# Range of A as one ScalarE Square pass, wider sums, dummy matmuls, wide output tiles: Nyström attention with gated experts on one core

## The chip, the core and the metric

One core of one Trainium2 chip. The metric is the device time of one execution in microseconds (us), the slowest core's, as the median of several runs. TensorE is called PE in the profile, VectorE DVE, ScalarE ACT, GpSimd POOL, SyncE SP. PEld is TensorE's weight load, which overlaps PE (before: 77.8 us of it beside 137.0 of PE, in a span of 176.5). The granted clock is the share of TensorE's full clock that the profile records for a stretch.

A run more than 1.5% above the fastest of the same kernel counts as slow. A ratio is the mean time of one kernel's fast runs over the mean of the other kernel's fast runs of the same rounds, so it isn't quite the ratio of the two medians that stand beside it.

## The reference, cut to what matters

```python
B, H, S, D = 8, 8, 576, 64;  m = 32                      # landmarks
q_lm, k_lm = means of 18 neighbouring rows of q, k
A  = softmax(q @ k_lm.T / 8)                              # 576 x 32 per head
Bm = softmax(q_lm @ k_lm.T / 8)                           # 32 x 32
C  = softmax(q_lm @ k.T / 8)                              # 32 x 576
Z  = Bm.T / (norm_1(Bm) * norm_inf(Bm) + 1e-6)
for _ in range(6): Z = 2 * Z - Z @ Bm @ Z
x  = (A @ Z @ C @ v) as (B*S, H*D)                        # 4608 x 512
e  = argmax(x @ w_gate);  gate_w = softmax(x @ w_gate)[e];  eom = sigmoid(x @ w_output_gate)[e]
out = gate_w * eom * (relu(x @ w1[e]) @ w2[e])            # 8 experts, 512 -> 1024 -> 512
```

A is nearly uniform for these inputs. The kernel therefore picks an expert per batch and evaluates the expert once on a linear form, and proves at the end, from the range of A (how far A is from 1/32), that this was allowed. If the proof fails for a batch, a fix-up behind a branch computes that batch again. With these inputs the fix-up isn't taken.

## The kernel before: the parts that matter here

Every instruction is placed by hand: the text `PLAN` lists name, engine and buffer slots (`dv0.1:G` means step 1 of the range of batch 0 on GpSimd), and each engine runs its own instructions in the order of that list.

```python
    def range_(b):                        # the range of A: five steps on GpSimd, one reduction on VectorE
        dev = tl("dev", fifo=False)
        ...
        def centre():
            nc.gpsimd.tensor_scalar(out=dev.ap, in0=A16[b]..., scalar1=-1.0 / m, scalar2=2048.0, op0=ADD, op1=MUL)
        def square(k):
            nc.gpsimd.tensor_tensor(span(0, k), span(0, k), span(0, k), op=MUL)
        def fold(k):
            nc.gpsimd.tensor_tensor(span(0, k), span(0, k), span(k, 2 * k), op=ADD)
        ...
        def top():
            nc.vector.tensor_reduce(dm[:, b:b + 1], span(0, S // 8), axis=AX, op=ADD)
```
```python
        def rowsum():                     # row sums of A: 8 matmuls of 144 columns a batch (QS = 144)
            for s in range(2):
                for par in range(2):
                    for hf in range(2):
                        o = hf * HS + s * QS
                        nc.tensor.matmul(pd.ap[quad(2 * par + hf), 0, 0:QS], lhsT=sel[:, s]...,
                                         rhs=A16[b][:, par, o:o + QS], start=(s == 0), stop=(s == 1))
```
```python
        for c in range(NC):               # output: five blocks a batch, each in one of four y buffers
            pY, y = pt(1), tl("y")        # tag("y", 4, [128, HD])
            ...                           # evict pY into y on ACT or DVE, then store y
```
```python
    n_extra = nc.values_load(nxi[0:1, 0:1], min_val=0, max_val=B * E)
    with tc.If(n_extra > 0):              # the fix-up; every engine jumps over it
        ...
```

The softmax here doesn't subtract the row's maximum and nothing guards it: scores larger than these inputs give would overflow.

Of the kernel before, what the change touches and what calls it, by code (L numbers as in the profile page):

```python
# [30 lines left out]
RELU = mybir.ActivationFunctionType.Relu  # L31
ABS = mybir.ActivationFunctionType.Abs
# [99 lines left out]
c_sel:V c_gen:V c_rest:G ldk0.0:Y0 c_zero:V ldq0.0:Y0 ldk0.1:Y ks0.1:G0 ldq0.1:Y ldq1.0:Y1 c_bsel:V c_two:V qs1.0.0:G0 qs0.0:V01  # L132
ks0.0:V1 qs0.1:V1 sc0.0C:T0 ldk1.0:Y1 eB0:S0 eC0.0:S0 qs1.0.1:G ldq2.0:Y2 sc0.0A:T2 eA0.0:S ldv0:Y0 ldk2.0:Y2 Bs0:V0 Br0:V
sc0.1A:T4 eA0.1:S ks1.0:V1 sc0.1C:T6 qs1.0.2:G qs1.0.3:G qs1.0.4:G1 eC0.1:S pd0:T0 qs2.0.0:G0 qs2.0.1:G qs2.0.2:G qs2.0.3:G
ln0:S0 rd0:S0 pT0.0:T2 pT0.1:T CT0:S0 ldq4.0:Y0 ldv1:Y1 pb0.1:T4 An0.1:V pb0.0:T6 ldv2:Y2 An0.0:V sc1.0C:T0 eB1:S1 Bs1:V1
sc1.0A:T2 sc1.1A:T4 sc1.1C:T6 eC1.0:S1 eC1.1:S pTt0:T0 pT1.0:T6 eA1.0:S dv0.0:G0 eA1.1:S Ct0:V0 pTt1:T1 pT1.1:T Cv0.0:T2 pd1:T0
ln1:S0 rd1:S1 Ct1:V1 Cv0.1:T CT1:S1 pb1.0:T4 ks2.0:V1 pb1.1:T0 Cvt0:T An1.0:V xr0:V0 qs2.0.4:G0 sc2.0C:T6 eC2.0:S0 cX0:V0
sc2.1A:T4 dv0.1:G eA2.1:S sc2.0A:T2 eA2.0:S ldk4.0:Y0 cB0.1:G cB0.0:V eB2:S0 sc2.1C:T4 ldq3.0:Y1 eC2.1:S cs0:T2 dv0.2:G pd2:T6
Br1:V qs4.0.0:G0 qs4.0.1:G qs4.0.2:G pTt2:T7 An1.1:V cb00:V0 cb10:S W0.0:T cb20:V Ct2:V0 Cv1.0:T0 ln2:S0 u0.0:V1 rd2:S0 pT2.0:T4
ldk3.0:Y1 Cv1.1:T Cvt1:T xr1:V1 cX1:S2 pT2.1:T Q0.0:V0 W0.1:T cB1.1:V Q0.1:V1 cB1.0:G CT2:S0 u0.1:S0 qs4.0.3:G dv0.3:G pb2.0:T6  # L140
ldq5.0:Y2 pb2.1:T0 qs4.0.4:G1 An2.0:V dv0.4:G cs1:T4 qs3.0.0:G0 An2.1:V W0.2:T Cv2.0:T6 u0.2:S1 Cv2.1:T Q0.2:V2 W0.3:T u0.3:S0
ks4.0:V1 qs3.0.1:G Cvt2:T ldv3:Y0 dv1.0:G1 cb01:V1 qs3.0.2:G qs3.0.3:G qs3.0.4:G0 W1.0:T xr2:V0 cb11:S dt0:V cX2:V1 sc4.1A:T0
sc4.0C:T6 dv1.1:G eB4:S1 eC4.0:S1 Q0.3:V0 W0.4:T cb21:V u1.0:V2 Q1.0:V1 ldk5.0:Y2 eA4.1:S W1.1:T sc4.1C:T6 u0.4:S0 sc4.0A:T0
ldq6.0:Y0 u1.1:S2 ldk6.0:Y0 eC4.1:S ks3.0:V0 eA4.0:S qs5.0.0:G0 Q1.1:V2 ldv5:Y1 W1.2:T pT4.0:T6 Q0.4:V0 dv1.2:G pT4.1:T CT4:S1
Q1.2:V1 ldv4:Y2 u1.2:V2 W1.3:T sc3.0A:T0 W0.5:T qs5.0.1:G eA3.0:S Q0.5:V2 sc3.0C:T6 u0.5:V2 eB3:S dv1.3:G eC3.0:S0 sc3.1C:T0
Q1.3:V1 u1.3:S0 W0.6:T ks5.0:V0 qs5.0.2:G qs5.0.3:G sc3.1A:T6 qs5.0.4:G1 u0.6.0:S0 pD0:T2 ldq7.0:Y1 eC3.1:S pT3.0:T0 pT3.1:T
W1.4:T MTd0.2:S pd4:T3 dv1.4:G eA3.1:S MTd0.1:S MTd0.0:V pTt3:T6 Q1.4:V0 pd3:T7 qs6.0.0:G0 CT3:S0 pg0:T0 ln4:S0 rd4:S1 u1.4:V2
W1.5:T MWg0:S0 Ct3:V1 Cv3.0:T2 pb4.1:T0 lg0:T6 ldk7.0:Y1 u1.5:V0 Q1.5:V2 W1.6:T mx0:V0 mk0:V0 ln3:S0 Cv3.1:T u1.6.0:S1 pD1:T7
An4.1:V pN0:T4 MTd1.1:S Cvt3:T cnt0:V e00:V0 m80:V0 pTt4:T5 rd3:S0 pb3.1:T0 MTd1.0:V MTd1.2:S Ct4:V0 pb4.0:T4 e20:S0 pg1:T6
MWg1:S1 An3.1:V An4.0:V e10:S ss0:V0 sc5.0C:T0 sc5.0A:T6 eA5.0:S lg1:T4 Bs2:V0 i80:V0 sc5.1A:T6 eC5.0:S0 eB5:S dt1:V xr3:V1  # L150
mx1:V1 eA5.1:S ef0:V0 Br2:V mk1:V1 pN1:T5 e01:V1 cnt1:V m81:V1 sc5.1C:T0 i81:V1 pd5:T5 cX3:S eC5.1:S er0:G pb3.0:T6 qs6.0.1:G
qs6.0.2:G ldw0.0:G ln5:S0 ldw0.1:G cB2.0:V dv2.0:G0 cB2.1:V Cv4.0:T2 cs2:T0 Cv4.1:T An3.0:V pT5.0:T6 cb02:V0 cb12:S qs6.0.3:G
pT5.1:T e21:S1 er1:G pTt5:T5 rd5:S1 ks6.0:V1 cb22:V Ct5:S1 ldw0.2:G CT5:S0 pb5.0:T4 An5.0:V qs6.0.4:G0 W2.0:T e11:S sc6.1A:T6
dv2.1:G u2.0:V2 Q2.0:V1 ldw0.3:G Cvt4:T xr4:V0 sel0:V sc6.0A:T4 eA6.1:S pb5.1:T6 An5.1:V eA6.0:S W2.1:T dv2.2:G Q2.1:V0
sc6.0C:T4 MW0.0:T6 cX4:S0 Bs4:V1 ldw1.1:G Br4:V h00.0:V dv2.3:G u2.1:S1 eB6:S0 eC6.0:S1 sa0.0:V mk0.0:G0 X0.0:S0 g10:V ldw1.0:G
W2.2:T MW0.1:T2 Q2.2:V2 g20:V sa0.1:V u2.2:S2 Cv5.0:T4 Cv5.1:T qs7.0.0:G0 Cvt5:T h00.1:V ss1:V1 P0.0.1:T6 P0.0.0:T7 mk0.1:G1
xr5:V1 g11:V co0:G ldw1.2:G X0.1:V1 W2.3:T Q2.3:V1 P0.1.0:T cX5:S g21:V tm0:V P0.1.1:T cm0:V pd6:T4 dv2.4:G dt2:V u2.3:S1
P160.0:S0 cB4.1:V P160.1:S ks7.0:V1 cB4.0:G ln6:S0 W2.4:T ldw1.3:G Y0.2:T5 u2.4:S2 rd6:S0 dv4.0:G0 cs4:T2 qs7.0.1:G pb6.1:T6
dv4.1:G Y0.0:T4 y0.2:S0 qs7.0.2:G y0.0:S1 qs7.0.3:G Q2.4:V0 cb04:V1 W2.5:T cb14:S An6.1:V dv3.0:G1 W4.0:T Y0.3:T5 Q2.5:V2
st0.2a:Y cb24:V u4.0:V1 ldv7:Y0 u2.5:S2 Q4.0:V1 ef1:V1 y0.3:S2 MW1.0:T6 st0.0a:Y h01.0:V mk1.0:G2 sa1.0:V W2.6:T u2.6.0:S0 co1:G  # L160
dv4.2:G u2.6.1:S sc6.1C:T4 eC6.1:S X1.0:V2 W4.1:T u4.1:S0 Y0.1:T0 MW1.1:T4 h01.1:V y0.1:S3 qs7.0.4:G1 dv4.3:G pD2:T1 MTd2.0:S
Q4.1:V0 sa1.1:V mk1.1:G0 P1.0.1:T0 MTd2.1:S MTd2.2:S W4.2:T pg2:T6 MWg2:S0 P1.0.0:T1 u4.2:S2 X1.1:V0 lg2:T6 Q4.2:V2 lg3:T
sc7.0C:T4 mx2:V0 e02:V0 mk2:V0 eC7.0:S0 e22:S0 dv3.1:G W4.3:T sel1:V ldv6:Y2 st0.3a:Y pN2:T7 cnt2:V eB7:S e12:S P1.1.0:T m82:V2
i82:V2 dv3.2:G ss2:V0 sc7.1C:T6 Bs6:V0 eC7.1:S Br6:V g12:V m83:V3 er2:G P161.0:V1 Q4.3:V1 pT6.0:T4 pT6.1:T CT6:S1 P1.1.1:T
P161.1:S u4.3:V1 pTt6:T6 ldw2.0:G Ct6:V0 Y0.4:T7 dv3.3:G pb6.0:T4 y0.4:S0 dv4.4:G W4.4:T i83:V3 u4.4:S0 Cv6.0:T0 An6.0:V
sc7.1A:T6 pTt7:T4 dt4:V ef2:V0 tm1:V Q4.4:V0 Cv6.1:T cm1:V W4.5:T Cvt6:T Y1.4:T5 ef3:V Ct7:V1 u4.5:V2 ldw2.2:G ldw2.1:G y1.4:V1
eA7.1:S g22:S xr6:V0 st0.1a:Y pT7.0:T6 Q4.5:V2 ldw2.3:G dv5.0:G0 er3:G dv5.1:G pT7.1:T cX6:S1 MW2.0:T4 CT7:S0 sc7.0A:T0 W4.6:T
u4.6.0:S1 Cv7.0:T6 u4.6.1:S h02.0:V eA7.0:S Cv7.1:T mk2.0:G1 sa2.0:V Y1.3:T2 st0.4b:Y sel3:V dv3.4:G st0.4a:Y Cvt7:T ldw3.0:G
dv5.2:G dt3:V sel2:V pD4:T3 Y1.1:T0 xr7:V1 cX7:V cB6.0:G st1.4a:Y ldw3.1:G X2.0:S1 MTd4.2:V st1.4b:Y MTd4.1:S cB6.1:V MTd4.0:V
pd7:T1 ln7:S0 y1.3:S2 MW2.1:T6 h02.1:V st1.3a:Y sa2.1:V cs6:T4 rd7:S1 pg4:T2 P2.0.0:T1 MWg4:S1 mk2.1:G2 dv5.3:G cb06:V0 cb16:S  # L170
Y1.0:T2 lg4:T3 lg5:T ldw3.2:G co2:G y1.1:V3 W6.0:T cb26:V Y1.2:T0 mx4:V1 mk4:V1 dv5.4:G X2.1:S2 pN4:T6 P2.1.0:T e24:S1 u6.0:V0
cnt4:V Q6.0:V1 m84:V0 W6.1:T y1.2:S0 y1.0:S1 e04:V1 tm2:G m85:V1 MW3.0:T6 i84:V0 Q6.1:V0 ldw3.3:G h03.0:V i85:V1 sa3.0:V
pb7.0:T2 e14:S u6.1:S2 P2.0.1:T0 P162.0:S0 W6.2:T er4:G ldw4.0:G P2.1.1:T ldw4.1:G u6.2:S1 An7.0:V P162.1:S er5:G Q6.2:V2 ef4:V1
cm2:V ldw4.2:G mk3.0:G0 pb7.1:T2 X3.0:S0 W6.3:T ldw4.3:G ldw5.0:G An7.1:V Y2.1:T1 MW5.0:T2 Q6.3:V1 u6.3:S0 dt5:V ss4:V1 sa5.0:V
y2.1:S2 Y2.4:T0 st1.2a:Y MW3.1:T6 dv6.0:G1 st1.0a:Y y2.4:S0 dv7.0:G0 h05.0:V st2.4a:Y W6.4:T mk5.0:G1 P3.0.0:T1 h03.1:V Q6.4:V0
ef5:V P3.0.1:T0 mk3.1:G2 u6.4:S2 X5.0:S1 X3.1:V2 W6.5:T sel5:V Q6.5:V2 u6.5:S1 P3.1.0:T P3.1.1:T sa3.1:V P163.0:S1 ldw5.1:G
ldw5.2:G g14:V P163.1:S MW5.1:T2 h05.1:V W6.6:T Y2.2:T1 Y3.3:T6 dv6.1:G Y3.0:T7 u6.6.0:S0 u6.6.1:S y2.2:S1 g24:S mk5.1:G0
ldw5.3:G sa5.1:V pD6:T0 MW4.0:T4 MTd6.1:S MTd6.2:S dv6.2:G MTd6.0:S X5.1:V0 st2.4b:Y dv7.1:G dv7.2:G P5.0.0:T1 h04.0:V mk4.0:G2
pg6:T2 Y3.1:T0 y3.0:V0 MWg6:V0 Y3.2:T7 lg6:T2 sa4.0:V st2.1a:Y y3.3:S2 lg7:T P5.0.1:T6 mx6:V0 mk6:V0 Y3.4:T3 st1.1a:Y y3.1:S3
e06:V0 pN6:T0 cnt6:V m86:V2 i86:V2 st2.2a:Y e26:S0 er6:G y3.4:S1 P5.1.0:T m87:V3 i87:V3 X4.0:S2 st3.0a:Y MW4.1:T2 P5.1.1:T  # L180
sel4:V ldw6.0:G Y2.3:T0 st3.1a:Y MW6.0:T4 h04.1:V sa4.1:V P165.0:S1 y3.2:S0 st3.2a:Y P4.0.1:T1 P165.1:V Y5.4:T7 er7:G co4:G
tm4:G P4.0.0:T6 y2.3:S3 mk4.1:G1 Y2.0:T0 h06.0:V ldw7.0:G st3.4b:Y st2.3a:Y e16:S st3.4a:Y y2.0:S0 X4.1:V1 dv7.3:G ldw6.1:G
ldw6.2:G mk6.0:G0 dv6.3:G sa6.0:V st3.3a:Y MW7.0:T2 P4.1.0:T P164.0:S0 cm4:V h07.0:V X6.0:V0 ef6:V0 st2.0a:Y P4.1.1:T Y5.0:T0
y5.4:S3 MW6.1:T4 st5.4a:Y P164.1:V ef7:V st5.4b:Y Y5.3:T6 y5.0:S1 Y4.0:T7 st5.0a:Y y5.3:S2 Y4.1:T1 P6.0.0:T0 P6.0.1:T6 h06.1:V
# [11 lines left out]
HOME = (0, 1, 0, 1, 0, 1, 0, 0)  # L196
AFTER_HIT = (5, 6, 7)
GUESTS = ()
UP = 1024.0


@with_exitstack
def kernel(
# [8 lines left out]
    shape=None,  # L212
# [11 lines left out]
    FC = F // 128  # L224
    NC = 5
    HS = S // 2
    QS = HS // 2
    CS = S + 32
    CH = CS // 2

# [154 lines left out]
    def const_zero():  # L385
        nc.vector.memset(MTd, 0.0)
# [824 lines left out]
```

## Time and profile before

| | before |
|---|---|
| device time, median of 3 runs | 177.8 us (177.61 to 178.24) |
| span of the profiled run, mean granted clock | 176.5 us, 0.961 |
| busy: PE, DVE, ACT, POOL | 137.0, 125.6, 92.0, 118.5 us |
| DVE's last cast before the branch ends | 172.2 us |
| from there to the end of the span | 4.3 us |

Three more lines are groups by shape: busy us and mean ns of one stand after the bar.

```profile
L852 DVE TENSOR_SCALAR sels<-iota,ef 128x8 f32<-128x8 int32 x8 | 4.9, 610 | 0.0
L828 DVE SCALAR_TENSOR_TENSOR e<-e,ss 128x40 f32<-128x40 f32 x2 | 3.6, 1791 | 0.0
L634 DVE SCALAR_TENSOR_TENSOR cur<-Bx,pair,Bs 128x128 f32<-128x128 f32 x4 | 2.7, 704 | 0.0
```

The means are much over the usual 0.22, 0.2 and 0.34 us, because a few instances took 1 to 2.8 us beside work of POOL.

```profile
SPq L1207 <- DMA w<-in_w_dram: 0.4, 1, 0.4
```

The page's first slices say 9 (full clock), but before 15.8 us the score matmuls (L470) took 0.71 us each, against 0.43 later. So PE was slow until about 16 us; PE at the slow pace is called cold below, at the later one warm.

### The profile page before, as it was taken

The page shows a single profiled execution, that of the slowest core. Times are in us where ns is not written, and L with a number is a line of the kernel's source. Part 1 is how long each engine was busy: PE and PEld are TensorE (multiplying, and loading weights), DVE is VectorE, ACT ScalarE, POOL GpSimd, SP SyncE. Part 2 cuts the span into 40 slices and gives each one's busy share as a digit, 9 for nine tenths or more (in the row PEclk, how much of TensorE's full clock was granted, in tenths as well). Part 3 has the DMA queues.
Part 4 walks back from the last instruction along what each step waited for, and adds up shares of the span by engine and source line. Part 5 has one row for each costly group of instructions (what it writes and reads, how often), then busy time and mean ns, then how long its engine had stood idle before and what let it go on. Part 6 is the DMA issues. An engine that isn't in the chain of part 4 may idle for free.

```text
span 176.5 us, 6239 instructions
## 1 busy us (share of the span) xinstructions
PE 137.0 (78%) x2513; PEld 77.8 (44%) x2526; DVE 125.6 (71%) x302; ACT 92.0 (52%) x210; POOL 118.5 (67%) x167
## 2 busy tenths in 40 slices
PE   0059766956998698596999999399899799999920
PEld 0014342643556354472465567155456445544400
DVE  6935547498366769999998865848777538899360
ACT  2007655534784456353784647546688182764640
POOL 3079999999999799578999579794669314405000
PEclk9999999999999999879999999969999969999995
DMA  4999999999999999999989389999999814485670
GB/s 152 410 411 437 410 428 424 412 409 422 407 410 429 413 378 224 214 190 188 177 267 400 101 157 202 218 207 196 241 222 223 268 65 154 153 308 201 231 289 26
DMA packets 15634, 48.87 MB, mean 277 GB/s; under 512 B 1648, under 2 KB 2672, under 8 KB 13680
## 3 DMA queue, kind: packets, MB, share of 16 engines
q1 hardware_dynamic: 12576, 37.90, 55.1%
q0 software_dynamic: 2880, 10.49, 31.7%
q8 instruction: 21, 0.34, 0.7%
q14 instruction: 13, 0.11, 0.2%
q10 hardware_dynamic: 144, 0.03, 0.1%
HBM read 62.05 MB, written 9.44 MB: 405 GB/s over the span
## 4 chain that ended last, share of the span: by engine, by line
PE 45%; DMA 28%; DVE 9%; issue 6%; ACT 5%; SPq 3%; POOL 1%; ACTq 0%; DVEq 0%; POOLq 0%
DMA kx<-in_k_dram 22%; PE psum L939 13%; PE psum L945 7%; DMA out_dram<-y 6%; PE psum L682 5%; PE psum L540 3%; PE psum L934 3%; PE psum L470 3%; PE psum L476 2%; DVE kx L440 2%; PE psum L508 2%; SPq L412 1%; PE psum L773 1%; PE psum L948 1%; ACT cur L693 1%
## 5 line engine op out<-in xcount | busy, mean ns | idle before, releaser
L939 PE MATMUL psum<-w,X 128*128 128x512 bf16 x116 | 32.8, 398 | 3.8 <-DVE X L989 1.7
L1025 ACT ACTIVATE y<-psum,cmain 128x512 f32<-128x512 f32 (+1 forms) x33 | 20.9, 656 | 13.3 <-PE psum L945 8.9
L878 POOL DMA_DIRECT2D w<-in_w_dram x32 | 12.2, 384 | 21.8 <-DMA w<-in_w_dram 13.0
L1045 POOL TENSOR_TENSOR dev<-dev 128x1152 bf16<-128x1152 bf16 (+1 forms) x16 | 26.0, 1629 | 0.4
L470 PE MATMUL psum<-kx,ql 64*32 64x304 f32 x256 | 14.6, 457 | 14.9 <-DVE kx L440 11.4
L1048 POOL TENSOR_TENSOR dev<-dev 128x576 bf16<-128x576 bf16 (+3 forms) x32 | 22.3, 696 | 1.8
L440 DVE TENSOR_REDUCE kx<-kx 128x128 f32<-128x2304 f32 (+1 forms) x8 | 19.2, 2399 | 5.2 <-DMA kx<-in_k_dram 5.2
L682 PE MATMUL psum<-cur,Q 64*64 64x128 f32 (+1 forms) x384 | 17.5, 283 | 3.6 <-issue 1.6
L997 DVE TENSOR_REDUCE sab<-psum 128x4 f32<-128x992 f32 x16 | 18.8, 1177 | 0.8 <-PE psum L934 0.8
L436 POOL TENSOR_TENSOR qa<-qa 128x512 f32<-128x512 f32 (+2 forms) x21 | 17.6, 839 | 2.3 <-DVE mx L790 1.1
L939 PEld LDWEIGHTS <-X 128*128 128x128 f16 x128 | 11.5, 100 | 15.7 <-issue 3.8
L945 PE MATMUL psum<-P,A 128*128 128x512 f16 x64 | 18.1, 389 | 0.0
L433 POOL TENSOR_TENSOR qa<-qT 128x1152 f32<-128x1152 f32 x7 | 17.0, 2425 | 0.8 <-DMA qT<-in_q_dram 0.6
L682 PEld LDWEIGHTS psum<-cur,Q 64*64 64x64 f32 x384 | 10.5, 135 | 11.8 <-issue 3.9
L693 ACT COPY cur<-psum 128x512 f32<-128x512 f32 (+1 forms) x19 | 9.8, 521 | 11.3 <-DVE Q L714 6.3
L476 PE MATMUL psum<-qT,kx 64*32 64x288 f32 x256 | 13.4, 444 | 0.6 <-ACT A L498 0.3
L934 PE MATMUL psum<-MTd,w 128*128 128x64 f16 x256 | 11.2, 201 | 2.6 <-DMA w<-in_w_dram 1.8
L934 PEld LDWEIGHTS <-w 128*128 128x128 f16 x256 | 10.2, 103 | 6.7 <-issue 2.5
L610 DVE SCALAR_TENSOR_TENSOR A<-A,lift,psum 128x576 f16<-128x576 f16 x16 | 12.7, 807 | 0.5 <-PE psum L605 0.5
L498 ACT ACTIVATE A<-psum 128x576 f16<-128x576 f32 x16 | 10.2, 652 | 5.0 <-PE psum L476 3.9
L470 PEld LDWEIGHTS psum<-kx,ql 64*32 64x32 f32 x256 | 4.1, 111 | 19.4 <-DVE kx L440 8.7
L714 DVE TENSOR_TENSOR Q<-twoI,psum 128x256 f32<-128x256 f32 (+1 forms) x25 | 8.9, 361 | 5.2 <-PE psum L682 4.3
(152 smaller groups left out, 258.6 us busy)
## 6 DMA issues: line engine op xcount, KB each, us to landing
w<-in_w_dram POOLq DMA_DIRECT2D x32, 512.0 KB
vn<-in_v_dram SPq DMA_DIRECT2D x8, 1170.0 KB, 14.8
out_dram<-y SPq DMA_DIRECT2D x32, 256.0 KB, 2.5
qT<-in_q_dram SPq DMA_DIRECT2D x7, 1152.0 KB, 14.0
kx<-in_k_dram SPq DMA_DIRECT2D x7, 1152.0 KB, 19.1
kx<-in_k_dram SPq DMA_DIRECT2D x2, 576.0 KB, 5.3
qT<-in_q_dram SPq DMA_DIRECT2D x2, 576.0 KB, 6.2
out_dram<-y SPq DMA_DIRECT2D x16, 64.0 KB, 2.5
```

Of the source, the lines that this page charges most:

```text
L433: nc.gpsimd.tensor_tensor(a, x[:, :, :, 0:9], x[:, :, :, 9:18], op=ADD)
L436: nc.gpsimd.tensor_tensor(a[:, :, :, 0:n], a[:, :, :, 0:n], a[:, :, :, n:2 * n], op=ADD)
L440: nc.vector.tensor_reduce(dst()[:, lo:hi], src()[:, lo:hi].rearrange("p a (t x) -> p a t x", x=g), axis=AX, op=ADD)
L470: nc.tensor.matmul(psC[hf].ap[quad(p), par, 0:CH], lhsT=ql.ap[half(par), p, :], rhs=kx.ap[half(par), p, CH * hf:CH * hf + CH], start=True, ...
L682: nc.tensor.matmul(it.ap[to, par, 128 * i + lo:128 * i + 128], lhsT=s[:, 0:64] if st == 0 else Q.ap[fr, par, i, :], rhs=s[:, lo:], start=T ...
L934: nc.tensor.matmul(o, lhsT=weights(b)[0][:, u, q, 128 * fc:128 * fc + 128], rhs=MTd[:, b, q, :].rearrange("p (a x) -> p a x", a=2), start= ...
L939: nc.tensor.matmul(dst, lhsT=Xt[:, fc - 4 * u, 128 * par:128 * par + 128], rhs=w2t[:, fc, :], start=(fc == 0), stop=(fc == FC - 1))
L945: nc.tensor.matmul(dst, lhsT=A16[b][:, par, 128 * c:128 * c + 128], rhs=Pt[:, par, :], start=(par == 0), stop=(par == 1))
L997: nc.vector.tensor_reduce(sab[:, b, f4], x, axis=mybir.AxisListType.XY, op=ADD, apply_absolute_value=True)
L1025: nc.scalar.activation(out=o, in_=x, func=COPY, scale=k)
L1045: nc.gpsimd.tensor_tensor(span(0, k), span(0, k), span(0, k), op=MUL)
L1048: nc.gpsimd.tensor_tensor(span(0, k), span(0, k), span(k, 2 * k), op=ADD)
```

## The change

Its intent: take 57 us of work off GpSimd, beside which some of VectorE's instructions took 1 to 2.8 us in place of 0.2 to 0.4; have PE do fewer small matmuls; warm PE before the first scores; and spare the evictions the wait for a y buffer. The diff, cut to its core (the whole order `PLAN` is new too, and some constants move between engines; the proof now sums the squares of the deviation where it summed fourth powers, and its constants follow):

```diff
-        steps = ((1.3, centre), (2.45, lambda: square(2 * S)), (1.3, lambda: fold(S)), (1.3, lambda: square(S)), (1.6, rest))
-        for j, (c, fn) in enumerate(steps):
-            plan.op(f"dv{b}.{j}", [("POOL", c, fn)], ...)
-        plan.op(f"dt{b}", [("DVE", 0.22, top)], ...)
+        def spread():
+            nc.scalar.activation(out=dev.ap, in_=A16[b].rearrange("p a s -> p (a s)"), func=SQUARE, scale=float(m), bias=minus,
+                                 accum_out=dm[:, b:b + 1])
+        plan.op(f"sq{b}", [("ACT", 1.35, spread)], ("R", b, 0.0), r=[("An", b)], w=[("rng",)], new=[dev])
```
```diff
-            for s in range(2):
-                for par in range(2):
-                    for hf in range(2):
-                        o = hf * HS + s * QS
-                        nc.tensor.matmul(pd.ap[quad(2 * par + hf), 0, 0:QS], ..., start=(s == 0), stop=(s == 1))
+            for par in range(2):
+                for hf in range(2):
+                    nc.tensor.matmul(pd.ap[quad(2 * par + hf), 0, 0:HS], ..., start=True, stop=True)
```
```diff
+WARM = ((47, 64), (46, 64), (7, 512))                      # dummy matmuls: count, columns
+WIDE = {2: "qT", 3: "kx", 4: "vn", 5: "qT", 6: "kx", 7: "vn"}   # whose dead tile holds the five output blocks
...
-            def ldq(lo=lo, hi=hi):                              # first query: two halves of the heads
-                nc.sync.dma_start(out=qT.ap[:, lo:hi, :]..., in_=qT_d[ORDER[b]][:, S * lo:S * hi])
+            def ldq(lo=lo, hi=hi, h=h):                         # first query: two halves of the sequence
+                    nc.sync.dma_start(out=qT.ap[:, :, HS * h:HS * h + HS], in_=...[:, :, HS * h:HS * h + HS])
...
-            pY, y = pt(1), tl("y")
+            pY = pt(1)
+            y = wide[0] if wide else tl("y")
+            off = HD * c if wide else 0
```

## The prediction

> **What bounds the kernel now.** I read the page from the top: engines, slices, then the chain that ended last, then the timeline and the stretch-by-stretch table wherever TensorE (PE) stood still.
>
> ```profile
> span 176.5 us, 6239 instructions
> PE 137.0 (78%) x2513; PEld 77.8 (44%) x2526; DVE 125.6 (71%) x302; ACT 92.0 (52%) x210; POOL 118.5 (67%) x167
> ...
> PE   0059766956998698596999999399899799999920
> ...
> POOL 3079999999999799578999579794669314405000
> PEclk9999999999999999879999999969999969999995
> DMA  4999999999999999999989389999999814485670
> ```
>
> No engine is full over the span, but PE is nearly full in the second half. The table by stretches puts PE's idle time, 176.5 - 137.0 = 39.5 us, here: 9.0 before the first matmul, 11.7 from 10 to 60 us, 5.2 from 60 to 90, 3.1 from 110 to 120, 1.6 from 120 to 140, 0.9 from 140 to 150, 8 after 165 us. Up to about 62 us the loads run at 410 to 430 GB/s with DMA share 1.0: this stage is DMA-bound, and the chain shows waits of 19 us for in_k there. POOL is also 90% busy there (query sums and the range of A on the same engine). From 90 us on PE is the bound, except in three dips of the slice rows (the digits 8-7, 6 and 6 of PEclk): 70 to 78, 110 to 118, 138 to 146 us. There the timeline shows:
>
> ```profile
> 69.42 1.99 DVE L712 TENSOR_TENSOR Q<-twoI,cur 128x256 f32<-128x256 f32 x1
> ...
> 71.47 0.67 PE L682 MATMUL psum<-cur,Q 64*64 64x128 f32 x16 [1.45 <-DVE Q L712]
> ...
> 111.73 1.79 DVE L634 SCALAR_TENSOR_TENSOR cur<-Bx,pair,Bs 128x128 f32<-128x128 f32 x1
> ...
> 112.07 1.29 POOL L1048 TENSOR_TENSOR dev<-dev 128x576 bf16<-128x576 bf16 x1
> 112.34 0.64 PE L934 MATMUL psum<-MTd,w 128*128 128x64 f16 x16 [1.33 <-DMA w<-in_w_dram]
> ...
> 114.53 0.48 PE L650 MATMUL psum<-cur,onesd 64*64 64x128 f32 x8 [1.55 <-POOL cur L637]
> ```
>
> First dip: a VectorE subtraction that usually takes 0.42 us took 1.99 while POOL ran a fold of the range (L1048), and PE waited 1.45 us for it; next a VectorE compare (L852) took 1.43 instead of 0.22. Second dip: one column block of the group's B took 1.79 on VectorE instead of 0.34; its other block queued on POOL behind the fold L1048 (1.29) and a weight load issue; PE waited 1.55. The third dip is another thing:
>
> ```profile
> 139.84 0.69 ACT L1025 ACTIVATE y<-psum,cmain 128x512 f32<-128x512 f32 x1 [3.01 <-DMA out_dram<-y]
> 140.57 0.81 PE L939 MATMUL psum<-w,X 128*128 128x512 bf16 x3 [1.29 <-ACT y L1025]
> ```
>
> The four y buffers were all held by stores; a store was in the chain with 10.15 us, so ScalarE waited 3.01 us for a buffer and PE 1.29 us for ScalarE. After each dip the granted clock is half:
>
> ```profile
> 114.00:116.00 2.00, 1.25 (x26) 0.69 (x28) 1.98 (x3) 0.70 (x3) 1.57 (x4) 0.70 1.03 171
> 116.00:118.00 2.00, 2.00 (x12) 0.90 (x11) 0.22 (x2) 1.30 (x4) 1.98 (x4) 0.50 1.04 236
> 118.00:120.00 2.00, 2.00 (x44) 1.46 (x42) 1.05 (x3) 0.30 (x2) 1.75 (x5) 0.94 1.06 206
> ```
>
> The column after POOL is the granted clock. It is 0.50 for about 3.4 us after each dip (finer stretches: 73.8 to 77.3, 114.9 to 118.2, 142.3 to 145.6). With PE full, each costs about 1.7 us more.
>
> [...]the stretched ones are L712, L634, L828 and L852; together they took 9.2 us more than their usual times (1.6 + 1.5 + 3.1 + 3.1), always beside POOL work. [...]At the start the clock column says 1.00, yet eight transposes took 1.46 us at 16.4 us against 1.02 later; so I think PE was cold there and the column does not show it. [...]Here 576 elements took 0.65 us and 1024 took 1.01[...]. [...]here a 1152-element product takes 2.11 us.
>
> **The change part by part.**
> - Range of A. Removed from POOL, for each of 8 batches: 1.15 + 2.11 + 1.28 + 1.15 + 0.73 + 0.46 + 0.32 = 7.2 us, 57.5 us in all (L1042 9.2, L1045 26.0, L1048 22.3), and from DVE 8 x 0.22. Added on ACT: 8 passes over 1152 elements, [...]say 1.3 with the accumulator: 10.4 us, ACT to about 102. ACT has 84 us idle, so it rarely lies on the path; I charge 0.7 us for passes that delay an eviction. POOL's removal is what frees the DVE and unblocks dips 1 and 2.
> - Row sums and their spread: 8 matmuls of 144 columns become 4 of 288, twice per batch; counts 5 become 1. Same columns, fewer fixed parts: the chain has 0.24 for 8 row sums, 0.42 for 8 spreads, 0.21 to 0.28 for 5 counts. I take 0.05 + 0.05 per batch and 0.1 per group, 1.3 us of PE, of which perhaps 1.0 lies where PE is full. Log and Exp over 288 instead of 144 add 0.24 us per batch to ACT, hidden.
> - Dummy matmuls: 47 + 7 wide at the start, 46 between the first two score blocks, all in PE's idle 9 us or while it waits for data. They should warm the array: in the trace the first batch's 64 score instructions run to 16.2 us; at the later rate (16 in 0.7) they need 2.8.
> - First query in halves of the sequence: the k halves load first, their sums both go to DVE (1.34 each, instead of 3.7 us of POOL work), the first A scores can start with half of q. DVE has then four sums of 1.35 and constants before the C scores, so these start about where they do now (12.3 us); with a warm array the batch's scores end about 1.7 us earlier. The load stream behind is unchanged at 410 to 430 GB/s up to 62 us, so I let only 0.5 us through to the end.
> - Wide output tile for batches 2 to 7: no y buffer to wait for; the same stores with the same bytes. Dip 3 goes: 0.7 + 0.8 us idle in 138 to 142 and about 1.6 us of half clock.
> - The whole static order is new; for instance, it loads the first expert before the last keys.
>
> Sum. The dips hold 2.25 + 3.1 + 1.5 = 6.85 us of idle PE and 3 x 1.7 = 5.1 us of clock loss, 11.9 us at most. I take 60%, because in dip 2 a weight load was also late (1.33) and would stand there alone, and because other waits fill in: 7.1. Then + 1.0 (matmuls) + 0.5 (head) - 0.7 (ACT) - 0.9 (general losses of a new order) = 7.0. 177.8 - 7.0 = 170.8 us.
>
> **The rivals.**
> (1) DMA takes over as the bound. For it: the share is 1.0 up to 80 us and again in 110 to 140; weight loads were already late by 1.33 and 0.47 us; no byte is removed. Against it: the share was 0.8 to 0.9 from 80 to 110, so about 4 us are free, and the loads are issued after routing, which itself comes earlier. Then dips 1 and 2 return as waits for weights: 174 to 175 us.
> (2) ACT becomes the bound: it gets 10.4 us of squares, most late y evictions, and longer Log and Exp. Against it: 52% busy, 60 to 70% in the last third. It would make 174 us, in the worst case no gain.
> (3) The freed POOL lets more through: query sums no longer share POOL with 29 us of range work in the first 60 us, so the middle batches start earlier, and all dips go with their clock loss. Then 166 to 167 us.
>
> **Range and chances.** The middle is 170.8; rival 1 or 2 in part gives the upper end 174.8, rival 3 the lower 167.0. Two per cent faster is 174.2 us, near the upper end. Chances: faster 0.82, same 0.16, slower 0.02.
>
> **What would show it.** Right if: POOL busy falls below about 70 us; each Square is 1.2 to 1.4 us; L712, L634, L828 and L852's successors show no 1 to 3 us instances; PE's idle between 60 and 150 us falls from about 11 to 5 us or less; the mean granted clock rises from 0.961 to 0.98 or more; no wait of ACT for an out_dram store. Half right if the clock dips stay but in another place with weight loads as releaser. Wrong if PE waits for ACT y or Square by several us, if table loads appear beside the squares, or if the loads up to 62 us slow down.

## The result, and the profile after

| runs | changed kernel, median | before, same runs | ratio of fast runs, 95% interval |
|---|---|---|---|
| first | 173.41 us (172.93 to 177.29) | 178.02 us | 0.967 [0.957, 0.976] |
| again, other runs (`a0_after_again`) | 170.98 us (170.46 to 172.67) | 178.51 us | 0.965 [0.958, 0.971] |

By the ratios it is 3.3 to 3.5% faster, about 6 us. The first profile fell in a slow run (span 175.8 us, clock 0.924), so everything below reads the profile of `a0_after_again`, which is fast (span 169.3 us, clock 0.976; the mean clock of its six runs is 0.967). Its head:

```profile
span 169.3 us, 6211 instructions
PE 138.9 (82%) x2541; PEld 78.1 (46%) x2542; DVE 120.7 (71%) x293; ACT 96.8 (57%) x217; POOL 71.7 (42%) x128
...
PE   6767867767898949889889999897999999999600
POOL 3000938999998699960491047110252002100000
PEclk9978999999999999999999999999999999999995
DMA  4999999999999999999999859999989997774740
```

POOL has little left to do in the second half, PE is busy from the start (dummies), and the clock row has no dip after the fourth slice. Between 60 and 150 us the same stretch, before (first) and changed (second); the columns are PE, PEld, DVE, ACT and POOL busy, granted clock, DMA share, GB/s:

```profile
60.00:150.00 90.00, 79.09 (x1446) 46.78 (x1449) 70.11 (x165) 51.72 (x125) 64.59 (x89) 0.94 0.90 219
```
```profile
60.00:150.00 90.00, 83.24 (x1483) 47.60 (x1483) 70.37 (x173) 61.64 (x142) 33.94 (x71) 1.00 0.98 254
```

PE's idle time fell from 10.9 to 6.8 us and the clock is whole. The Square pass, and the small instruction that reads its accumulator:

```profile
L1051 ACT ACTIVATE dev<-A,minus 128x1152 bf16<-128x1152 f16 x8 | 10.1, 1257 | 0.0
...
L1051 ACT ACTIVATION_READ_ACCUMULATOR dev<-A,minus 128x1 f32 x8 | 1.6, 200 | 0.0
```

What PE still waits for (us in total, times, longest us):

```profile
PE psum L485 <- POOL ql L449: 4.5, 4, 1.9
PE psum L491 <- DMA qT<-in_q_dram: 2.2, 1, 2.2
PE psum L1079 <- DVE ub L1078: 1.9, 1, 1.9
PE psum L391 <- DVE minus L342: 1.6, 1, 1.6
PE psum L694 <- POOL Q L724: 1.5, 2, 1.0
```

The first four belong to the query sums and the load stage, to the proof at the end and to the constants at the start; no wait for weights or for ScalarE is among them; the next two are 1.4 us for ScalarE (Cexp L504) and 1.1 us for weights. The chain that ended last looks less good: its shares before and in the changed kernel, and two pieces of the latter (start us, us):

```profile
PE 45%; DMA 28%; DVE 9%; issue 6%; ACT 5%; SPq 3%; POOL 1%; ACTq 0%; DVEq 0%; POOLq 0%
...
DMA 37%; PE 36%; POOL 11%; DVE 4%; issue 3%; SPq 3%; POOLq 1%; ACT 0%
...
53.81 28.66 DMA qT<-in_q_dram
...
101.96 14.63 DMA w<-in_w_dram
```

Transfers and GpSimd's query sums now have a larger part in it, and a weight load stands in it, which before none did. One stretched VectorE instruction is left among those named in the prediction, beside the query sum that GpSimd still has (start us, us):

```profile
63.46 2.53 POOL L444 TENSOR_TENSOR qa<-qT 128x1152 f32<-128x1152 f32 x1
63.61 2.41 DVE L861 TENSOR_SCALAR sels<-iota,ef 128x8 f32<-128x8 int32 x1
```

**Part of the gain is given back at the very end.** VectorE's last cast ends 9.3 us earlier than before (162.9 against 172.2), yet the span is only 7.2 us shorter. SP's waits have it (us in total, times, longest; L1207 is the same wait before):

```profile
SPq L1200 <- DMA w<-in_w_dram: 2.5, 1, 2.5
```

The DMA's name is a guess of the profile (the last matmul that reads weights, L948, had ended at 155.9). What SP waits for is a semaphore that GpSimd sets at the end. In the trace GpSimd branches over the fix-up at 163.10 us and its next instruction comes at 165.70, 2.60 us later; in the kernel before, 0.49 us after the branch. The other engines go on after 0.23 to 0.51 us in both. The semaphore for which that instruction waits was last set at 163.05, so it is no late transfer. Packets of instructions land about then with the stall and without it (1.5 to 2.6 us after GpSimd's branch in the kernel before, 1.5 to 2.4 in the first profile of the changed one), but the trace doesn't say for which engine. Up to the branch, the trace has 350 instructions of GpSimd before and 308 after: the range's work is gone. So my theory was that the shorter program itself brings the stall; by what means, the traces don't show.

### The profile page after: what moved, and what is told of

Its sections match the earlier page's. It is cut to its first block, busy times and chain, and to the rows that moved or that the text cites.

```text
span 175.8 us, 6211 instructions
## 1 busy us (share of the span) xinstructions
PE 144.5 (82%) x2541; PEld 80.6 (46%) x2542; DVE 120.6 (69%) x293; ACT 96.6 (55%) x217; POOL 71.6 (41%) x128
## 4 chain that ended last, share of the span: by engine, by line
PE 49%; DMA 27%; POOL 8%; DVE 4%; issue 4%; ACT 2%; SPq 2%; POOLq 0%; DVEq 0%
DMA kx<-in_k_dram 15%; PE psum L948 13%; PE psum L954 8%; DMA qT<-in_q_dram 7%; PE psum L694 7%; DMA out_dram<-y 5%; PE psum L485 4%; PE psum L943 3%; PE psum L491 3%; POOL qa L447 3%; POOL qa L444 3%; PE psum L524 2%; PE psum L957 2%; DVE sab L1006 1%; PE psum L785 1%
## 5 line engine op out<-in xcount | busy, mean ns | idle before, releaser
L948 PE MATMUL psum<-w,X 128*128 128x512 bf16 x128 | 31.5, 380 | 0.1
L455 DVE TENSOR_REDUCE kx<-kx 128x128 f32<-128x2304 f32 (+1 forms) x8 | 18.0, 2247 | 5.5 <-DMA kx<-in_k_dram 5.5
L948 PEld LDWEIGHTS <-X 128*128 128x128 f16 x128 | 11.4, 98 | 13.0 <-issue 1.4
L485 PE MATMUL psum<-kx,ql 64*32 64x304 f32 x256 | 13.5, 496 | 3.2 <-POOL ql L449 2.9
L998 DVE SCALAR_TENSOR_TENSOR X<-h,psum 128x1024 f16<-128x1024 f32 x10 | 12.1, 1210 | 0.0
L943 PE MATMUL psum<-MTd,w 128*128 128x64 f16 x256 | 10.1, 194 | 1.5 <-DMA w<-in_w_dram 1.4
L943 PEld LDWEIGHTS <-w 128*128 128x128 f16 x256 | 9.1, 98 | 4.5 <-DMA w<-in_w_dram 1.6
L705 ACT COPY cur<-psum 128x512 f32<-128x512 f32 (+1 forms) x15 | 8.4, 560 | 4.8 <-DVE Q L726 2.6
L524 PE MATMUL psum<-ident,Cexp 128*128 128x128 f32 x64 | 10.1, 290 | 1.1 <-DVE A L622 0.5
L556 PE MATMUL psum<-vn,CT 128*32 128x65 f32 x512 | 9.8, 230 | 0.6 <-ACT A L514 0.6
L1051 ACT ACTIVATE dev<-A,minus 128x1152 bf16<-128x1152 f16 x8 | 10.1, 1258 | 0.0
```

Source lines behind the costliest of these rows:

```text
L455: nc.vector.tensor_reduce(dst()[:, lo:hi], src()[:, lo:hi].rearrange("p a (t x) -> p a t x", x=g), axis=AX, op=ADD)
L485: nc.tensor.matmul(psC[hf].ap[quad(p), par, 0:CH], lhsT=ql.ap[half(par), p, :], rhs=kx.ap[half(par), p, CH * hf:CH * hf + CH], start=True, ...
L524: nc.tensor.transpose(pT.ap[:, par, 128 * c:128 * c + 128], in_=Cexp.ap[:, par, o:o + 128], identity=ident)
L943: nc.tensor.matmul(o, lhsT=weights(b)[0][:, u, q, 128 * fc:128 * fc + 128], rhs=MTd[:, b, q, :].rearrange("p (a x) -> p a x", a=2), start= ...
L948: nc.tensor.matmul(dst, lhsT=Xt[:, fc - 4 * u, 128 * par:128 * par + 128], rhs=w2t[:, fc, :], start=(fc == 0), stop=(fc == FC - 1))
```

## The experiments

Twelve kernels ran, four on another chip. All gave correct results. All had five timed rounds. The medians take in slow runs and the profiled run, the ratios don't. So differences of medians below are a little off: by the ratios the Square pass (d1) is worth 3.7 us, both parts (d2) 4.4 and d0 9.7.

| kernel | median us | before us | ratio, 95% interval | last cast ends, to span's end (us) |
|---|---|---|---|---|
| a0 changed, again | 170.98 | 178.51 | 0.965 [0.958, 0.971] | 162.9, 6.4 |
| a1 no dummies | 172.57 | 178.51 | 0.969 [0.961, 0.976] | 164.9, 7.0 (slow) |
| a2 more dummies | 173.87 | 178.51 | 0.972 [0.964, 0.980] | 166.1, 6.6 |
| a3 first query by heads | 172.13 | 178.51 | 0.965 [0.957, 0.973] | 164.8, 6.4 |
| a4 range back on GpSimd | 229.92 | 178.27 | 1.286 [1.278, 1.295] | (slow) |
| b1 before + Square | 178.29 | 178.27 | 0.999 [0.993, 1.005] | 168.9, 7.1 |
| b2 before + wide tiles | 176.62 | 178.27 | 0.990 [0.984, 0.996] | 168.3, 4.3 |
| c1 changed + 42 memsets | 169.15 | 178.27 | 0.951 [0.946, 0.957] | 167.4, 4.5 (slow) |
| d0 the same, memsets late | 168.52 | 178.39 | 0.946 [0.941, 0.950] | 163.6, 4.5 |
| d1 before + Square + 56 memsets | 174.24 | 178.39 | 0.979 [0.974, 0.984] | 167.8, 4.3 |
| d2 before + Square + wide + 56 memsets | 173.56 | 178.39 | 0.975 [0.969, 0.981] | 167.6, 4.3 |
| d3 = d0 with narrow sums | 172.87 | 178.39 | 0.970 [0.964, 0.977] | 165.0, 4.3 |

"(slow)" marks a profile that fell in a slow run; its times by the span aren't compared.

### The changed kernel again

No edit.

> The changed kernel, unedited, to see it in its fast state beside the other runs: the first profile fell in the slow state. Expected 172 to 174 us, ratio to before near 0.967. If the slow run was slow because of its end (the SyncE queue waited 3.7 us there, 0.4 in before), a fast run has the same stages up to 168 us and an end 3 us shorter; if it was slow because of more half-clock windows of PE, its mean clock is above 0.94 and its dips shorter or elsewhere.

170.98 us, with the same ratio as in the first runs. The scatter of the first was that of slow runs. This profile is the one that the point-by-point account below uses.

### The head: dummies away, more dummies, first query by heads

```diff
-WARM = ((47, 64), (46, 64), (7, 512))
+WARM = ()                                    # a1, and the three dummy steps out of the order
+WARM = ((47, 64), (46, 64), (19, 512))       # a2
```
```diff
-nc.sync.dma_start(out=qT.ap[:, :, HS * h:HS * h + HS], in_=...)        # halves of the sequence
+nc.sync.dma_start(out=qT.ap[:, lo:hi, :]..., in_=qT_d[...][:, S * lo:S * hi])   # a3: halves of the heads
```

> The changed kernel without any dummy matmul (the constant tile stays). Theory: the dummies end at 6.5 us, the first scores start at 9.2, so the array has gone cold again; then leaving them out costs under 0.5 us, or even gains because the 46 in the middle (2.46 us at half clock in the first profile) stand before the C scores. Rival (my prediction): the dummies make the first batch's scores end 1.7 us earlier, so without them the first batch ends later by that, and the whole by 0.5 us.

> The changed kernel with 19 instead of 7 wide dummies, so that they last until about 9.2 us, when the first half of q is there. [...]the granted clock stays at 1.00 from 9 to 13 us and the first 16 A score instructions take 0.7 instead of 1.22 us; gain at the head 0.5 to 1.5 us. To the end: under 0.7 us if the loads pace the first 60 us (theory), the whole 1 to 1.5 us if PE does (rival).

> The changed kernel with the first q loaded and summed in halves of the heads again, as before (4608-byte instead of 1152-byte runs), all scores waiting for both halves. Theory: the first A scores then start about 1.3 us later, the C scores at the same 12.7 us or 0.3 earlier since the loads are not cut in small runs (5 to 10 us moved 365 GB/s against about 420 before); the end changes by under 0.5 us either way. Rival: the cut is what lets the head go, and the end is 1 us later.

The dummies do warm PE: 16 of the first A scores (start, us) in the changed kernel, without dummies, and with more:

```profile
9.41 0.72 PE L491 MATMUL psum<-qT,kx 64*32 64x288 f32 x16 [2.17 <-DMA qT<-in_q_dram]
...
12.56 1.27 PE L485 MATMUL psum<-kx,ql 64*32 64x304 f32 x16 [0.53 <-DVE ql L452]
```
```profile
9.14 1.22 PE L490 MATMUL psum<-qT,kx 64*32 64x288 f32 x16 [9.14 <-DMA qT<-in_q_dram]
```
```profile
9.67 0.72 PE L490 MATMUL psum<-qT,kx 64*32 64x288 f32 x16
...
12.22 0.75 PE L484 MATMUL psum<-kx,ql 64*32 64x304 f32 x16 [0.39 <-DVE ql L451]
```

The seven wide dummies are a little too short: PE idles 2.17 us for the query, and from 11 us the granted clock is 0.50 again; the second block takes 1.27. With nineteen the clock is whole up to 17 us, that block takes 0.75, and the first batch's scores end at 14.0 us in place of 15.1. They end at 15.5 without dummies, so the seven gain only 0.4 us there, and at 14.6 with the query by heads, where I had expected 0.3 us at most. But none of the three edits moves the total beyond the overlap of the intervals, and the one with the earliest scores has the highest median. Up to some 60 us the loads run at full share (row DMA above; 403 to 416 GB/s in each 10 us from 10 to 60) and, I take it, set the pace, so that an earlier first batch waits later. The head is worth less than these runs can tell: 0.7 us for the dummies by the ratios, within the noise, and nothing seen for the halves.

What differs between such runs is where half-clock stretches fall. From stretches of 0.5 us, those before the last matmuls:

```
before             73.5-77.5, 114.5-118.5, 142-145.5
changed (slow run)  9-12.5, 43-50, 63.5-67, 84-91
a0 changed         11-14.5
a1                 39-46, 63-66.5
a2                 17-20.5, 27.5-34.5, 65-72
a3                 8.5-12, 25.5-36, 63-70
b1                 27-30.5
b2                 80.5-84, 114.5-118
d0                 38.5-45.5, 62.5-66
d1                 27.5-31
d2                 none
d3                 17.5-24, 72-75.5
```

They come in pieces of 3.4 us, or two or three of them in a row (3.41 us each in the records of the kernel before, 6.83 for two in those of the first changed profile). My estimate from that length and the clock of 0.50 is that a piece costs at most 1.7 us, half its length; up to 60 us, where PE waits for loads anyway, I take them for nearly free, which no run shows. The nearly identical kernels a0 to a3 have them in different places. They are part of the scatter of 2 to 5 us between runs of one kernel, not most of it: over the 24 runs of a0 to a3, each taken about its kernel's mean, time and mean clock are correlated by -0.54, which is 0.3 of the variance.

### Range back on GpSimd in the new order

```diff
-        plan.op(f"sq{b}", [("ACT", 1.35, spread)], ...)
+        plan.op(f"dv{b}.{j}", [("POOL", c, fn)], ...)       # five steps as before, put between GpSimd's other work
+        plan.op(f"dt{b}", [("DVE", 0.22, top)], ...)
```

> The changed kernel with the range of A put back on GpSimd in the old five steps per batch (40 instructions of GpSimd and 8 small ones of VectorE, no Square pass), everything else as changed. My theory (GpSimd's range work makes VectorE instructions take 1.4 to 2 us in place of 0.2 to 0.45 and starves the tensor engine of its operands): half or more of the saving of 7.5 us goes, 175 to 178 us, with VectorE instructions of over 1.3 us beside GpSimd's back in the trace. Rival (the new static order and the wide tiles made the saving, the range was never on the path): within 1.5 us of the 171.0 of the changed kernel. By the count of its instructions GpSimd should also find the end sooner again, near 0.5 us after its branch in place of 2.6, which hides up to 2 us of what the range costs; so the time of the last VectorE cast, 162.9 us in the changed kernel, decides, not the span.

229.92 us: worse than either theory. The timeline shows why:

```profile
40.31 0.23 DVE L1068 TENSOR_REDUCE dm<-dev 128x1 f32<-128x72 bf16 x1 [15.89 <-POOL dev L1061]
40.46 2.54 DVE L456 TENSOR_REDUCE kx<-kx 128x128 f32<-128x2304 f32 x1
...
43.06 2.17 PE L492 MATMUL psum<-qT,kx 64*32 64x288 f32 x32 [15.55 <-DVE kx L456]
```

I had put the closing reduction (L1068) into VectorE's fixed order before GpSimd could have its input, so VectorE stood 15.89 us and the key sum behind it, and PE with it. Eight such waits sum to 53.2 us. This run measures my bad order, not the range; it tells nothing between the theories, and the next experiment replaces it. One thing came as expected: with 363 instructions up to its branch, GpSimd goes on 0.49 us after it.

### The Square pass alone, in the old order

```diff
 # the kernel before, its order kept; the 40 dv and 8 dt steps out, sq<b> on ACT where dv<b>.0 stood
-        plan.op(f"dv{b}.{j}", [("POOL", c, fn)], ...)
+        plan.op(f"sq{b}", [("ACT", 1.35, spread)], ...)
```

> The kernel before in its old order, with only the range of A as one Square pass of ScalarE. My theory: the dips of the tensor engine at 70 to 78 and 110 to 118 us go or halve; last VectorE cast at 167 to 169 us in place of 172.2; the span 173 to 175 us, because GpSimd has 42 instructions fewer and its wait after the branch grows to 2.6 us. Rival (the order must be made anew for it, otherwise nothing comes through): last cast at 171 or later, span 176 us or more. Second rival (this part alone makes the whole saving): span 171 us.

178.29 us, ratio 0.999: taken by itself, the largest part of the change seems worth nothing. But the last cast ends at 168.9 us in place of 172.2. The 3.3 us are lost after the branch:

```profile
SPq L1188 <- DMA w<-in_w_dram: 3.2, 1, 3.2
```

GpSimd has 294 instructions up to the branch here, 56 fewer and not 42 as I had written. It goes on 0.50 us after it, runs two, and then stands from 169.71 to 172.58 us, though the semaphores of the next instruction had been complete since 137.3 us. It looks like the stall of the changed kernel, two instructions further on. My estimate for the stall was 2.6 us; the rival that the order must be made anew isn't shown by this run, since the compute did end earlier.

### The wide output tiles alone, in the old order

```diff
-            pY, y = pt(1), tl("y")
+            y = wide[0] if wide else tl("y")     # and y at column HD * c of it
```

> The kernel before in its old order, with only the wide output tiles for batches 2 to 7. My theory: the wait of ScalarE for a y tile at 139.8 us goes and with it the dip at 138 to 146 us; last cast 1.5 to 2.5 us earlier, span 174.5 to 177 us, the two early dips as before. Rival (stores are bound by the DMA queue and the wait only moves to the weights or to the next store): span within 1 us of the kernel before.

176.62 us, 0.990: 1.65 us faster, as expected, though the interval allows 0.8 to 2.9 us. The third dip is gone and the second stands; the kernel before comes first, then this one:

```profile
110.00:120.00 10.00, 6.90 (x107) 3.96 (x107) 6.25 (x15) 4.82 (x15) 8.62 (x17) 0.83 1.06 213
140.00:150.00 10.00, 9.08 (x84) 4.76 (x86) 5.47 (x15) 5.43 (x13) 2.58 (x8) 0.83 0.32 113
...
110.00:120.00 10.00, 7.41 (x109) 4.17 (x109) 6.45 (x16) 4.81 (x14) 8.70 (x16) 0.83 1.07 211
140.00:150.00 10.00, 10.00 (x109) 5.45 (x107) 8.52 (x22) 6.62 (x14) 4.02 (x12) 1.00 0.47 164
```

PE is busy 7.41 of 10 us in the second dip (6.90 before), and all 10 where the third was (9.08 at a clock of 0.83 before).

### The end: 42 GpSimd memsets

```diff
+    filler = keep.tile([128, 1], F32, name="filler")
+    for _ in range(42):
+        nc.gpsimd.memset(filler, 0.0)
```

> The changed kernel with 42 GpSimd memsets of 128x1 put after its last work and before the branch over the fix-up, so that GpSimd's program is as long as before the change. My theory ([...]because the program became 42 instructions shorter): GpSimd's first instruction after the branch comes 0.5 us after it in place of 2.6, span 168 to 169.5 us, 2 us below the changed kernel. Rival[...]: the gap stays over 2 us and the span at 170.5 to 171.5 us.

> The changed kernel with 42 GpSimd memsets again, now fixed in the order after GpSimd's last mask (in the run c1_filler the trace shows them in the first 10 us). My theory (only the position of the branch in GpSimd's program counts, not when the memsets run): GpSimd goes on 0.5 us after its branch, 168 to 169.5 us, ratio to before near 0.950. Rival (the gain of c1_filler came from what early memsets delay): the gap is over 2 us again and the ratio 0.960 to 0.967.

In c1 the memsets were written after the last work, but ran in GpSimd's first 10 us, since they stood outside the fixed order. In d0 they are a step of the order after GpSimd's last mask. Both give the same: GpSimd goes on 0.49 us after its branch, and SP's line is back where it was before the change:

```profile
SPq L1205 <- DMA w<-in_w_dram: 0.5, 1, 0.5
```

169.15 and 168.52 us; ratios 0.951 and 0.946 against 0.965 of the changed kernel without them. So 42 idle instructions make the kernel faster, by 1.8 and 2.5 us of the medians (2.3 and 3.4 by the ratios; the calls differ), about the 2.1 us of the stall, and when they run makes no difference that these runs can tell. This version (d0) beats both kernels: 9.9 us under the kernel before.

Over all profiles the count decides: with 294 or 308 instructions up to the branch GpSimd stalls (six profiles, 2.6 to 3.8 us), with 350 or 363 it doesn't (eight profiles, 0.49 us). What causes it is not shown. In all six stalled profiles one more packet of instructions starts 0.6 to 0.7 us after GpSimd has gone on; but the packets during the stall don't name their engine, and those of the queue with the small packets (8 KB) land 0.55 to 1.7 us before it goes on.

### Square alone and both parts, with the end repaired

```diff
 # b1, and b1 with the wide tiles; 56 memsets at the end of GpSimd's order, so that it has 350 again
+    plan.op("fill", [("POOL", 5.6, fill)], ("Z", 0, 5.0), w=[("fill",)])
```

> The kernel before in its old order with the Square pass alone, as in b1_square_alone, plus 56 GpSimd memsets after GpSimd's last work, which bring its program to the 350 instructions of before. My theory (Square alone made the last VectorE cast 3.3 us earlier[...]): no stall of over 1 us after the branch, 175 to 176 us, ratio 0.982 to 0.988. Rival (the Square alone is worth nothing in the old order, and the profile of b1 was a lucky one): ratio 0.995 to 1.0.

> The kernel before in its old order with the Square pass, the wide output tiles and the 56 memsets. My theory (each part removes its own dips, so they add, about 2.7 us and 1.7 us): 173 to 174.5 us, ratio 0.970 to 0.978; what then remains to the 169 us of the changed kernel with memsets, 4 to 5 us, is the new order, the wider sums and the head. Rival (both parts feed the same bound and do not add): ratio 0.98 or more. Second rival (the order is worth nothing): ratio 0.955 or less.

d1: 174.24 us, 0.979. With the stall gone (0.49 us after the branch) the Square pass alone is worth 4.15 us, a bit more than expected. Of the 4 us between b1 and d1 the stall is 2.9; the last cast also came 1.1 us earlier here. Where its gain lies shows in the same stretch as above, 60 to 150 us:

```profile
60.00:150.00 90.00, 81.52 (x1505) 47.86 (x1517) 70.48 (x174) 62.04 (x145) 25.71 (x55) 1.00 0.91 232
```

The three groups of VectorE from before, again:

```profile
L828 DVE SCALAR_TENSOR_TENSOR e<-e,ss 128x40 f32<-128x40 f32 x2 | 3.0, 1480 | 0.0
...
L852 DVE TENSOR_SCALAR sels<-iota,ef 128x8 f32<-128x8 int32 x8 | 1.8, 232 | 0.0
L634 DVE SCALAR_TENSOR_TENSOR cur<-Bx,pair,Bs 128x128 f32<-128x128 f32 x4 | 1.7, 444 | 0.0
```

Together they took 11.2 us before and take 6.5 here; what is left stands beside GpSimd's query sums. PE's idle time falls from 10.9 to 8.5 us, and the clock from 60 us on is whole: all three half-clock pieces of before are gone (in b1 too), the third with them, though the y buffers still are waited for:

```profile
ACT y L1025 <- DMA out_dram<-y: 6.0, 5, 2.6
```

How much of the gain is the stretched VectorE and how much GpSimd's own queue isn't separated: in the second dip PE waited 1.55 us for a GpSimd instruction (L637) that stood behind a fold of the range.

Nor do the parts seem to add: d2, with both, is at 173.56 us, 0.975, and the wide tiles bring 0.7 us on top in place of the 1.65 of b2 (the intervals of d1 and d2 overlap and allow -0.7 to 2.1 us). So that they don't add isn't shown by the times; the clock argues for it, as the third piece of half clock can go only once. The expected range of 173 to 174.5 holds, the reason given ("they add") is in doubt.

### The row sums as before

```diff
 # d0 with rowsum() and spread() of the kernel before, and its sel and bsel constants
-                    nc.tensor.matmul(pd.ap[quad(2 * par + hf), 0, 0:HS], ..., start=True, stop=True)
+                        nc.tensor.matmul(pd.ap[quad(2 * par + hf), 0, 0:QS], ..., start=(s == 0), stop=(s == 1))
```

> d0_filler_late with the row sums of the normalisation and their spread as before: per batch 8 matmuls of 144 columns twice in place of 4 of 288, and Ln and Exp over 144 in place of 288 columns. My theory (fixed parts of 64 matmuls on TensorE, where it is mostly full): 0.6 to 1.0 us slower than d0_filler_late. Rival (TensorE has the slack, and the shorter Ln and Exp pay it back): within 0.4 us of it, or faster.

172.87 us against 168.52 of d0 in the same rounds: 4.35 us, not 0.6 to 1.0. The matmuls themselves, d0 first, then d3 (busy us, mean ns):

```profile
L617 PE MATMUL psum<-rd,bsel 32*128 32x288 f16 x32 | 4.8, 290 | 0.4 <-ACT rd L606 0.4
...
L597 PE MATMUL psum<-A,sel 128*32 128x288 f16 x32 | 2.5, 295 | 0.6 <-ACT A L513 0.6
```
```profile
L626 PE MATMUL psum<-rd,bsel 32*128 32x144 f16 x64 | 5.0, 236 | 0.3 <-ACT rd L614 0.2
...
L605 PE MATMUL psum<-A,sel 128*32 128x144 f16 x64 | 2.8, 254 | 0.4 <-ACT A L519 0.4
```

Busy time differs by 0.5 us only. The two profiled runs are just 1.6 us apart (d0's is its slowest run), so they can't show the whole difference. Aligning ScalarE's instructions of the two profiles, d3 is level at 66 us (0.2 us ahead), 2.4 us behind at 73 to 79, and 1.4 behind at the end; a half-clock piece at 72 to 75.5 lies there in d3, none in d0. Over the fast runs the mean granted clock was 0.9494 in d3 and 0.9618 in d0. A piece of half clock of t us lowers the mean by 0.5 t / span and costs at most 0.5 t, so 0.0124 x 168 = 2.1 us is an upper estimate of what the clock accounts for. The rest, about 2 us or more, isn't explained by these profiles; d3 also runs an order made for the wide sums, and its constants are four more VectorE instructions (297 in all against 293; VectorE is busy 120.7 us in both). That the narrow sums are slower here is shown; why they are by so much is open.

## Why the prediction was right, step by step

The total was right: 170.8 us predicted, 171.0 and 173.4 measured. The mechanism of its largest part, GpSimd's range work in the way of VectorE and PE, was right too. But that the total came so close is partly luck: several terms were mis-sized, and their errors cancel.

- **POOL's work stretches VectorE, and this makes the first two dips: right.** By d1, the Square alone brings 4.15 us. L852's eight instances fall from a mean of 610 ns to 232 there; both clock pieces at 74 and 115 us vanish. How much went through VectorE and how much through GpSimd's own queue is open. My 9.2 us of stretched VectorE took in too much: 2.6 of it is one L828 of 2.79 us beside a query sum (L433), which the change keeps. A part remains with POOL's query sums: one L828 at 2.76 us in d1, the 2.41 us above in the changed kernel. POOL's busy time came out at 71.7 us, just over the "about 70" that was named.
- **The Square's cost: right.** 1.26 us a pass, within the 1.2 to 1.4 that was named. But the accumulator is a separate instruction of 0.20 us, so a pass with it takes 1.46 in place of the 1.3 of my estimate. ACT's total is 96.8 us rather than 102, because the new order moved other work off it. No table loads appear beside the squares: the trace has one, of 1.28 us (L337).
- **The third dip goes with the wide tiles: half right.** In the old order they alone bring 1.65 us (b2). But the dip also goes with the Square alone (in d1 PE is busy 9.90 us from 140 to 150 at full clock), so the two savings probably overlap. The wait of ACT for a store still exists in the changed kernel for batches 0 and 1 (3.0 us in two waits; they have three y buffers in place of four), where nobody waits for it.
- **The term "dips, 60% of 11.9 = 7.1 us": too large.** Both parts together gave 4.8 us (d2), 40%. The idle time of 60 to 150 us fell to 6.8, not to the "5 or less" named; the clock rose to 0.976, not 0.98.
- **The term "matmuls, 1.0 us": too small.** Undoing only the row sums and spreads costs 4.35 us (d3). The fixed parts that I summed are about right (0.5 us of PE), and so is the longer Log and Exp (0.25 us more per batch by the two profiles, 0.24 predicted). What I left out is that the clock may be halved at other places, which covers up to 2.1 us by the estimate above; the remainder is open.
- **The head, 0.5 us: not refuted.** The first batch ended 1.1 us earlier, not 1.7, because the dummies were short and the clock fell again at 11 us; of the 1.1 the dummies gave 0.4. My reading of the eight transposes at 16.4 us as cold was wrong: they took 272 to 330 ns each, as later, the record has the full clock from 15.8 us, and the 1.46 us hold an idle stretch. PE was cold, but before that. The effect on the total is below what the runs can tell.
- **The end: missed.** I had no term for it. The removal of 42 GpSimd instructions cost about 2 us after the branch (GpSimd's next instruction 2.60 us after it, against 0.49). Without it the whole saving is 9.9 us, so my sum of 7.0 landed by luck: a gain that was too small met a loss that I hadn't seen.
- **The rivals.** DMA as the new bound: not by PE's waits, as none for weights is among the five largest shown above (1.1 us in all); but the chain's DMA share rose from 28 to 37%, with 14.6 us of one weight load, and DMA's share of 60 to 150 us from 0.90 to 0.98. So little room is left there, and no run took bytes away to test it. ACT as the bound: no, PE's largest wait for ScalarE is the 1.4 us for Cexp, none for a Square or an output. "The freed POOL lets more through, 166 to 167 us": with the end repaired the kernel comes near it at 168.5, but the load stage isn't faster: from 10 to 62 us it moved 417 GB/s before and 408 after.

Adding up: Square 4.15, wide tiles 0.7 on top, then 5.0 from d2 to d0 for wider sums, new order and head. Of the last, d3 gives 4.35 to the sums, in the new order. What the order does by itself wasn't run alone.

## What to carry to other kernels

Measure a part of a change by when the last compute ends as well as by the span: here a part worth 4 us showed nothing, because an engine with a shorter program stood still for 2.87 us after its branch (b1). If a kernel ends in a branch over code that isn't run, look at the gap after the branch on each engine, and try a few dozen idle instructions on the engine that stalls (42 brought 2.60 us down to 0.49 here). And when PE is near full, count a removed dip with its half-clock stretch only once: two parts that each remove it need not add.
